# A self-planned attention and convolution kernel: ties between GpSimd and VectorE, zero matmuls in TensorE's gaps, and another schedule

## The chip, the cores and the metric

One NeuronCore of one Trainium2 chip. The metric is device time of the whole kernel in microseconds (us), the median of several executions. The kernel before took 180.95 us (179.91 to 183.62) when it was first timed.

## The reference, cut to what matters

```python
def _attn_ref(r, k, v, w, u):                 # B,H,S,D = 4,8,768,48
    for t in range(S):
        cur = np.einsum('bhd,bhe->bhde', u[None] * kt, vt)
        y[:, :, t] = np.einsum('bhd,bhde->bhe', rt, state + cur)
        state = wt[:, :, :, None] * state + np.einsum('bhd,bhe->bhde', kt, vt)

def _moe_ref(x, w_proj, filter_fft, w_out):   # x: attention's output, 4 x 768 x 384
    x1, x2, x3 = split(x @ w_proj, 3)
    x2_conv = irfft(rfft(x2) * rfft(filter_fft))      # along the sequence
    return (x1 * x2_conv * x3) @ w_out
```

Inputs are float32. The kernel computes in bfloat16 and accumulates in float32.

## The kernel before

The attention runs in 24 chunks of 128 time steps (4 batches of 6). Chunks are loaded in groups of one or two. After the six chunks of a batch comes its convolution, as discrete Fourier transforms by matmul. All four batches interleave: while TensorE transforms batch 0, the chunks of batch 1 and 2 go through.

The order of the instructions is not written by hand. Each step is an `Op` with a due time, a modelled cost for each engine that can do it, and a flag `lock`. A greedy planner chooses at each step the operation that can start first, and the kernel then emits the instructions in planned order. `lock` marks VectorE operations with two inputs in SBUF and all GpSimd operations: in the *plan* they exclude each other through the variable `port`. Nothing in the emitted program enforced that. There each engine runs its own list and waits only for its data.

```python
def dve(n, lock=False):
    h = n / 960.0 + 0.069
    return (DVE, h, h + 0.09, lock)
def pool(n, h=None):                                   # GpSimd always takes the lock
    h = h or n * 0.00228 + 0.08
    return (POOL, h, h + 0.06, True)
...
    def order(self):                                   # the planner, cut
        free = {PE: 0.8, ACT: 0.8, DVE: 0.8, POOL: 0.8, SP: 0.8}
        while ready:
            ...
                    est = max(free[e], t0 + hop, port if lock else 0.0)
            ...
            est, o, (e, hold, lat, lock), got = best
            if e == PE and est < COLD:
                hold, lat = 2 * hold, lat + hold       # half clock at the start
            o.eng, free[e], o.end = e, est + hold, est + lat
            if lock:
                port = est + hold
            ...
            out.append((est, o, e, {k: held[k] for k in o.one + o.two + o.uses}))
        return out
```

Four kinds of operation:

```python
# rk: product of r and k of a group (GpSimd or VectorE); its transposes and rx follow on TensorE
op(f"rk{gi}", T(i0, O_RK), [pool(n * C), dve(n * C, True)], lambda e, bk: mul(
    e, rk[f][:, 0:n], kr[sl][:, 1, 0:n], kr[sl][:, 0, 0:n]), r=[f"r.{sl}", f"k.{sl}"], w=[f"rk.{f}"])
# vc: v times a bonus per head (GpSimd or VectorE)
op(f"vc{gi}", T(i0, O_VC), [pool(n * C, 0.78 * n), dve(n * C, True)], ...)
# kq: VectorE, one input in PSUM, one in SBUF: no lock
op(f"kq{i}", T(i, O_KH), [dve(2 * C)], ...)
# U0..U3: products of a spectrum X with the filter's spectrum HR, HI, HG: two SBUF inputs, lock
op(f"pr{b}.{nm}.{lo}", d, [dve2(C * (hi - lo), True)] + ([pool(C * (hi - lo))] if nm in ("U1", "U3") and PP else []), ...)
...
    with tc.manual_schedule(engines={E.PE, E.Activation, E.DVE, E.Pool, E.SP}):
        for est, o, e, bk in plan.order():
            o.fn(e, bk)
```

Of the kernel before, what the change touches and what calls it, by code (L numbers as in the profile page):

```python
# [11 lines left out]
BF16 = mybir.dt.bfloat16  # L12
INT32 = mybir.dt.int32
AF = mybir.ActivationFunctionType
# [6 lines left out]
L = 128  # L21
# [8 lines left out]

PE, ACT, DVE, POOL, SP = "PE", "ACT", "DVE", "POOL", "SP"

PACE = 4.317
S2O0, S2O1, S2O2, S2O3 = 20.744, 8.77, 13.518, 14.093
S2S0, S2S1, S2S2, S2S3 = 28.784, 29.661, 40.0, 9.432
TAB, FIL, TBL = 13.024, 20.0, 7.203
WP1, WP2, WP3 = 4, 2, 4
WO, FL = 9, 3
NM, PP = 11, 1
O_MA = 7  # L40
O_MC = 5.088
COLD, TIE, PB, AB, PS = 16.0, 0.51, 1.078, 0.313, 11.871
HOP = 0.07
NP = 3
NS1 = 8 - 2 * NP
SLACK = {PE: 0.032, ACT: 0.020, DVE: 0.079, POOL: 0.014, SP: 0.0}
NBP = 10
NLD, NF, NG, NS, NO = 4, 4, 2, 2, 6
LEAD, OUTD, OUTG = -8.347, 0.5, 5
BONUS = "p" * NBP + "d" * (13 - NBP)  # L50
O_LN = 1.65
O_VB = 4.7
O_RK = 3.425
O_RKU = 5.0
O_CC = 4.43
O_RT = 2.335
O_RX = 4.34
O_CP = 1.1
O_VC = 5.289
O_CSI = -1.17  # L60
O_EN = -0.078
O_KH = 0.092
O_TR = 5.123
O_QK = 5.028
O_SC = 3.04
O_MT = 5.712
O_KV = 3.636
O_SU = 3.17
O_Y = 5.164
O_XN = 7.724  # L70
O_YT = 5.514
O_XT = 5.9
O_SD = 7.149


def act(n, sb=False):
# [33 lines left out]
class Plan:  # L110
# [43 lines left out]
            av[best[1]] = 1e9  # L154
        return t, got

    def order(self):
        free = {PE: 0.8, ACT: 0.8, DVE: 0.8, POOL: 0.8, SP: 0.8}
        port, dma = 0.0, 0.0
        avail = [0.0] * (self.npairs + self.nsingles)  # L160
        held, last, moves, out = {}, {}, [], []
        for o, k in self.after:
            o.preds.add(self.named[k])
        for o in self.ops:
            o.left = len(o.preds)
            o.wait = [p for k in o.one + o.two for p in self.gate.get(k, ()) if p is not o and k not in p.uses]
            for p in o.preds:
                p.succs.append(o)
        ready = [o for o in self.ops if not o.left]
        while ready:  # L170
            best, cands = None, {}
            for o in ready:
                t0 = max((p.end for p in o.preds), default=0.0)
                got = {}
                if o.one or o.two:
                    if any(p.eng is None for p in o.wait):
                        continue
                    at = self.place(o, avail)
                    if at is None:
                        continue  # L180
                    t0, got = max(t0, at[0]), at[1]
                opts = []
                for x in o.engs:
                    e, hold, lat, lock = x
                    hop = HOP if got or any(p.eng != e for p in o.preds) else 0.0
                    est = max(free[e], t0 + hop, port if lock else 0.0)
                    for k in o.uses:
                        if last[k][1] != e:
                            est = max(est, last[k][0] + HOP)
                    opts.append((est + lat - (min(PB, max(0.0, o.due + PS - est)) if e == POOL else AB if e == ACT else 0.0), est, x))  # L190
                fin = min(opts, key=lambda q: q[0])[0]
                for f, est, x in opts:
                    if f <= fin + TIE:
                        cands.setdefault(x[0], []).append((est, o, x, got))
            for e, cs in cands.items():
                m = min(c[0] for c in cs)
                pick = min((c for c in cs if c[0] <= m + SLACK[e]), key=lambda c: (c[1].due, c[0]))
                if best is None or pick[0] < best[0]:
                    best = pick
            est, o, (e, hold, lat, lock), got = best  # L200
            ready.remove(o)
            if e == PE and est < COLD:
                hold, lat = 2 * hold, lat + hold
            o.eng, free[e], o.end = e, est + hold, est + lat
            if lock:
                port = est + hold
            if o.bus:
                if e == SP:
                    dma = max(dma, est + 1.2) + o.bus
                    o.end = dma + 0.8  # L210
                    moves.append(o)
                else:
                    start = est + 1.4
                    for m in moves:
                        if m.end - 0.8 > start:
                            m.end += o.bus
                    dma = max(dma, start) + o.bus
                    o.end = start + o.bus + 0.3
            for k in o.two + o.one:
                held[k] = got[k]  # L220
                avail[got[k]] = 1e9
            for k in o.uses:
                self.users[k] -= 1
            for k in o.one + o.two + o.uses:
                last[k] = (max(last.get(k, (0.0, e))[0], o.end), e)
            out.append((est, o, e, {k: held[k] for k in o.one + o.two + o.uses}))
            for k in o.one + o.two + o.uses:
                if self.users[k] == 0 and k in held:
                    avail[held.pop(k)] = last[k][0]
            for s in o.succs:  # L230
                s.left -= 1
                if not s.left:
                    ready.append(s)
        assert len(out) == len(self.ops)
        return out


# [5 lines left out]
def kernel(  # L243
# [12 lines left out]
    nc = tc.nc  # L256
# [50 lines left out]
    mask_neg = sb.tile([L, L], BF16, name="mask_neg")  # L307
    ident = sb.tile([L, L], BF16, name="ident")
    ones = sb.tile([L, 1], BF16, name="ones")
    scl0 = sb.tile([L, 1], FP32, name="scl0")  # L310
    u_f = sb.tile([L, H, D], FP32, name="u_f")
    u_b = sb.tile([L, H, D], BF16, name="u_b")
# [15 lines left out]
        return pairs[bk[n]]  # L328

    def mul(e, o, a, b):  # L330
        (nc.vector if e == DVE else nc.gpsimd).tensor_mul(o, a, b)  # L331

    def copy(e, o, a):
        if e == ACT:
            nc.scalar.activation(out=o, in_=a, func=AF.Copy)  # L335
        else:
            (nc.vector if e == DVE else nc.gpsimd).tensor_copy(out=o, in_=a)  # L337

    def halves_of(x):
        v4 = x.rearrange("p (a q c) -> p a q c", q=2, c=L)  # L340
# [10 lines left out]
    def maps(e, bk):  # L351
# [15 lines left out]
            )  # L367
        nc.gpsimd.memset(fmap[:, L:L + 1], float(HALF))

    def pads(e, bk):  # L370
        nc.vector.memset(ones, 1.0)
        for t in lg:
            nc.vector.memset(t[:, :, :, D:DP], 0.0)
        for t in kq:
            nc.vector.memset(t[:, :, :, D:DP], 0.0)
# [18 lines left out]
            )  # L394

    op("masks", -9, [(POOL, 1.5, 1.6, True)], masks, w=["masks"])
    op("pads", -9, [(DVE, 0.75, 0.85, False)], pads, w=["pads"])
    op("smalls", -8, [(DVE, 0.16, 0.25, False)], smalls, w=["smalls"])
    op("table", -9, [(ACT, 1.283, 1.283, False)],
       lambda e, bk: nc.scalar.preload_act_table_set("natural_log_exp_and_others"), w=["table"])  # L400
# [489 lines left out]
                second(b)  # L890

    E = mybir.EngineType
    with tc.manual_schedule(engines={E.PE, E.Activation, E.DVE, E.Pool, E.SP}):
        for est, o, e, bk in plan.order():
            o.fn(e, bk)


# [28 lines left out]
```

## Time and profile before

| | before |
|---|---|
| time, first timing | 180.95 us, 3 runs |
| span of the profiled run | 178.5 us |
| TensorE busy | 151.0 us (85%) |
| VectorE busy | 137.8 us (77%) |
| ScalarE / GpSimd busy | 129.4 / 60.2 us |
| TensorE gaps over 0.25 us, summed from the trace | 20.7 us: 13.7 before 37 us, 6.15 between 60 and 120 us |
| half clock on record | 36.4 to 43.2 us |

In the profile PE is TensorE's matmuls, PEld its weight loads, DVE is VectorE, ACT ScalarE, POOL GpSimd and SP SyncE. The rows of 40 digits cut the span into equal slices, each digit a busy share in tenths; PEclk is the granted TensorE clock in tenths of full. A line of the timeline gives start, duration, engine, source line, operation, output <- inputs, and in brackets how long the engine stood idle before it and what it waited for.

The chain of work that ended last, by engine:

```profile
PE 61%; DVE 18%; ACT 9%; DMA 5%; issue 3%; POOL 1%; SPq 1%; ACTq 0%; DVEq 0%; POOLq 0%
```

VectorE holds 18% of the path to the end, so it is not only TensorE that binds. And two groups of VectorE instructions by source line (count, then shortest/median/longest in ns, first and last start in us, forms):

```profile
L827 DVE TENSOR_TENSOR y<-eo,g x12: 541/550/1830, 88.3 to 170.3; 128x768 bf16<-128x768 bf16 x12
L798 DVE TENSOR_TENSOR U<-X,HI x11: 345/739/2109, 79.1 to 163.8; 128x1152 bf16<-128x1152 bf16 x6, 128x384 bf16<-128x384 bf16 x5
```

One form, with a median of 550 ns and a longest of 1830 ns: the longest met GpSimd (it is one of the pair of y at 112.56 us, while two vc ran on GpSimd from 111.2 to 114.4 us). I summed over the trace how much each VectorE instruction exceeds the lower quartile of its form, counting excesses over 0.06 us. The result, 5.3 us, is called *VectorE's excess* below. It compares within one trace, and so it misses a form that occurs once. There is such a case, a fourth collision, with GpSimd's rk beside a plain copy:

```profile
74.63 1.81 POOL L331 TENSOR_TENSOR rk<-kr 128x768 bf16<-128x768 f32 x1 [6.10 <-DMA kr<-in_r_dram]
74.88 1.68 DVE L696 COPY HG<-HI 1x384 bf16<-1x384 bf16 x1 [0.21 <-ACT HI L693]
```

In b_zeros and b_ties3 (below) the same copy takes 0.25 us. With it before's excess is 6.7 us. The copies of HG are planned as part of an operation of ScalarE, so neither `lock` nor the ties know of them.

### The profile page before, as it was taken

Reading aid. Unit: us, or ns where it says so; the run is one execution under the profiler, and the core shown is the slowest. Engines: PE = TensorE matmul, PEld = TensorE weight load, DVE = VectorE, ACT = ScalarE, POOL = GpSimd, SP = SyncE. Lnnn points to the kernel's source line nnn. Section 1 sums busy time; section 2 is a strip of 40 time slices with the busy share of each in tenths; the row PEclk is TensorE's granted clock in tenths of the full one; section 3 lists DMA queues with packets and bytes.
Section 4 is the critical chain, followed back from the end, with each engine's and each line's share of the span. In section 5 each row is a group of like instructions: output and inputs, shape, how many; then the busy total and the mean of one; then the engine's idle time right before and its main releaser. Section 6 shows DMA issues by size and latency. Waiting matters only on the chain.

```text
span 178.5 us, 4574 instructions
## 1 busy us (share of the span) xinstructions
PE 151.0 (85%) x1806; PEld 96.8 (54%) x1806; DVE 137.8 (77%) x249; ACT 129.4 (72%) x218; POOL 60.2 (34%) x71
## 2 busy tenths in 40 slices
PE   0639778779999799897999689799999999999850
PEld 0419556566676576473456356466676675555220
DVE  3798677545547789899969999968898899579720
ACT  4599887774798766998778767989866874647440
POOL 6542745740632713220418006804710341002000
PEclk9999999956999999999999999999999999999997
DMA  6999798999999999899998999124000000001515
GB/s 121 202 202 214 140 209 176 200 196 200 229 189 200 317 182 210 176 183 198 212 227 172 210 305 210 34 88 180 4 0 4 0 4 0 0 0 56 214 59 208
DMA packets 106054, 26.45 MB, mean 148 GB/s; under 512 B 100528, under 2 KB 106032, under 8 KB 106032
## 3 DMA queue, kind: packets, MB, share of 16 engines
q1 hardware_dynamic: 104432, 24.98, 64.1%
q0 software_dynamic: 1600, 1.18, 4.6%
q8 instruction: 14, 0.23, 0.6%
q14 instruction: 8, 0.07, 0.1%
HBM read 22.61 MB, written 4.72 MB: 153 GB/s over the span
## 4 chain that ended last, share of the span: by engine, by line
PE 61%; DVE 18%; ACT 9%; DMA 5%; issue 3%; POOL 1%; SPq 1%; ACTq 0%; DVEq 0%; POOLq 0%
PE pair L724 7%; PE pair L762 6%; PE pair L647 5%; DVE U L798 5%; PE pair L841 4%; PE single L724 4%; PE single L511 4%; ACT pair L498 3%; PE pair L523 3%; PE pair L586 3%; DMA w<-in_w_dram 3%; PE pair L640 2%; PE pair L813 2%; DVE kq L503 2%; DMA kr<-in_r_dram 2%
## 5 line engine op out<-in xcount | busy, mean ns | idle before, releaser
L331 POOL TENSOR_TENSOR rk<-kr 128x768 bf16<-128x768 f32 (+1 forms) x13 | 22.0, 1695 | 17.4 <-DMA kr<-in_r_dram 17.4
L503 DVE TENSOR_TENSOR kq<-pair,kr 128x768 bf16<-128x768 f32 x24 | 22.6, 951 | 3.8 <-PE pair L586 1.9
L543 POOL TENSOR_SCALAR_AFFINE_SELECT mt<-mt 128x512 bf16<-128x512 bf16 x11 | 7.0, 638 | 52.7 <-ACT mt L335 46.5
L498 ACT ACTIVATE pair<-pair 128x768 f32<-128x768 f32 x24 | 19.3, 804 | 4.3 <-PE pair L494 4.0
L724 PE MATMUL pair<-xT,wproj 128*128 128x384 bf16 x96 | 18.1, 326 | 0.0
L331 POOL TENSOR_TENSOR vc<-vb,cc 128x768 bf16<-128x768 bf16 (+1 forms) x9 | 12.3, 1372 | 17.1 <-ACT cc L335 8.6
L724 PEld LDWEIGHTS <-wproj 128*128 128x128 bf16 x144 | 12.5, 97 | 9.4 <-issue 2.7
L535 DVE TENSOR_TENSOR mt<-pair,mask_excl 128x1024 bf16<-128x1024 f32 x13 | 15.8, 1214 | 1.1 <-PE pair L523 1.1
L762 PE MATMUL pair<-wproj,sd 128*128 128x384 bf16 x72 | 14.7, 343 | 0.0
L841 PE MATMUL pair<-wout,y 128*128 128x384 bf16 x72 | 13.2, 326 | 1.6 <-DVE eo L824 0.8
L335 ACT ACTIVATE ab<-pair 128x768 bf16<-128x768 f32 x12 | 9.7, 812 | 6.4 <-PE pair L762 6.4
L335 ACT ACTIVATE X<-pair 128x768 bf16<-128x768 f32 x12 | 9.7, 810 | 6.4 <-PE pair L647 5.2
L335 ACT ACTIVATE xn<-pair 128x384 bf16<-128x384 f32 x24 | 11.8, 491 | 3.1 <-PE pair L586 2.5
L491 PE MATMUL pair<-lg,mask_neg 128*128 128x384 bf16 x24 | 8.3, 346 | 6.4 <-ACT lg L439 4.2
L511 PEld LDWEIGHTS <-kq 128*128 128x128 bf16 x192 | 12.9, 106 | 1.3 <-issue 0.6
L439 ACT ACTIVATE lg<-w 128x768 bf16<-128x768 f32 (+1 forms) x13 | 10.4, 797 | 3.3 <-DMA w<-in_w_dram 3.3
L335 ACT ACTIVATE o<-pair 128x768 f32<-128x768 f32 x12 | 9.4, 810 | 4.3 <-PE pair L841 4.2
L724 PE MATMUL single<-xT,wproj 128*128 128x384 bf16 x48 | 10.4, 325 | 1.8 <-DVE xT L337 1.6
L511 PE MATMUL single<-ident,kq 128*128 128x128 bf16 x128 | 10.3, 225 | 0.3 <-ACT x L335 0.3
L335 ACT ACTIVATE ev<-pair 128x384 f32<-128x384 f32 x12 | 5.9, 490 | 6.4 <-PE pair L814 6.4
L540 DVE TENSOR_TENSOR mt<-pair,mask_excl 128x512 bf16<-128x512 f32 x11 | 7.6, 687 | 3.7 <-PE pair L523 2.3
L523 PE MATMUL pair<-qk 48*128 48x128 bf16 x192 | 9.9, 227 | 0.5 <-ACT qk L335 0.3
(132 smaller groups left out, 380.2 us busy)
## 6 DMA issues: line engine op xcount, KB each, us to landing
w<-in_w_dram SPq DMA_DIRECT2D x24, 192.0 KB, 4.1
kr<-in_k_dram SPq DMA_DIRECT2D x24, 192.0 KB, 4.6
kr<-in_r_dram SPq DMA_DIRECT2D x24, 192.0 KB, 3.9
v<-in_v_dram SPq DMA_DIRECT2D x24, 192.0 KB, 3.7
out_dram<-o SPq DMA_DIRECT2D x12, 384.0 KB, 3.3
U<-in_moe_filter_fft_dram SPq DMA_DIRECT2D x1, 1152.0 KB, 7.1
wproj<-in_moe_w_proj_dram POOLq DMA_DIRECT2D x3, 288.0 KB, 5.7
wout<-in_moe_w_out_dram POOLq DMA_DIRECT2D x1, 288.0 KB, 5.8
```

The source lines that it names most:

```text
L331: (nc.vector if e == DVE else nc.gpsimd).tensor_mul(o, a, b)
L335: nc.scalar.activation(out=o, in_=a, func=AF.Copy)
L439: op(f"ln{gi}", T(i0, O_LN), [act(n * C, True)], lambda e, bk: nc.scalar.activation(out=lg[f][:, 0:n, :, 0:D], in_=wl[sl][:, 0:n], func=AF ...
L498: nc.scalar.activation(out=p[:, :, 0:C], in_=p[:, :, 0:C], func=AF.Exp)
L503: op(f"kq{i}", T(i, O_KH), [dve(2 * C)], lambda e, bk: nc.vector.tensor_mul(kq[f][:, :, :, 0:D], two(bk, f"cs{i}")[:, :, 0:C].rearrange("p ...
L511: nc.tensor.transpose(p[:, HP * m + j, :], kq[f][:, m, 2 * j:2 * j + 2, :], ident)
L523: nc.tensor.matmul(p[:, par, j, :], qk[f][p0:p0 + D, j, :], qk[f][p0:p0 + D, HP + j, :], start=True, stop=True,)
L535: op(f"mt{i}", T(i, O_MT), [dve(1024)], lambda e, bk: nc.vector.tensor_mul(mt[s2_], scored(bk, 0, 2), _mid(mask_excl, H)), r=["masks"], w= ...
L647: nc.tensor.matmul(p, F[:, ti, c0:c0 + L], x[:, ti, :], start=(ti == 0), stop=(ti == NT - 1),)
L724: nc.tensor.matmul(p, wproj[:, cb, col0:col0 + L], xT[bx][:, cb, sl], start=(cb == 0), stop=(cb == CB - 1),)
L762: nc.tensor.matmul(two(bk, n)[:, q, 0:C], sd[q][:, cb, ti * L:(ti + 1) * L], wproj[:, cb, C:2 * C], start=(cb == 0), stop=(cb == CB - 1),)
L841: nc.tensor.matmul(two(bk, n)[:, z, 0:C], y[cb][:, t0:t0 + L], wout[:, cb, :], start=(cb == 0), stop=(cb == CB - 1),)
```

## The change

It has three parts. The planner now fills planned TensorE gaps of over 0.7 us with matmuls on a tile of zeros, meant to keep TensorE busy enough for its full clock (*zeros*: 29 matmuls in four places). At emission, a GpSimd instruction is made to wait for the last VectorE instruction that the plan has finished by its start (*ties*: in the new order, GpSimd instructions with a wait for VectorE go from 12 to 41, as the prediction counted). A tie holds one direction only: no VectorE instruction is made to wait for a GpSimd one. And the planner's constants were searched anew with both in place, which gives another interleaving (*order*). The diff, cut to its core:

```diff
-PACE = 4.317
+PACE = 3.8
+WARM = 0.7
-COLD, TIE, PB, AB, PS = 16.0, 0.51, 1.078, 0.313, 11.871
+COLD, TIE, PB, AB, PS = 5.0, 0.439, 0.991, 0.313, 12.0
-NBP = 10
-NLD, NF, NG, NS, NO = 4, 4, 2, 2, 6
+NBP = 11
+NLD, NF, NG, NS, NO = 3, 3, 2, 2, 6
 ... (some 30 more constants of the same kind)
+            if e == PE and est > free[PE] + WARM:
+                step = 0.43 if free[PE] < COLD else 0.22
+                idle = [i for i in range(self.npairs, len(avail)) if avail[i] <= free[PE]]
+                if idle and est - free[PE] > step + 0.1:
+                    n = int((est - free[PE] - 0.1) / step)
+                    x = Op("warm", 0, [(PE, n * step, n * step, False)], warm(n), (), (), (), 0.0)
+                    x.end = free[PE] + n * step
+                    out.append((free[PE], x, PE, {"warm": idle[0]}))
...
+    def warm(n):
+        def fn(e, bk):
+            for _ in range(n):
+                nc.tensor.matmul(one(bk, "warm"), wt[:, 0:L], wt, start=True, stop=True)
+        return fn
+
     def pads(e, bk):
+        nc.vector.memset(wt, 0.0)
...
-        for est, o, e, bk in plan.order():
-            o.fn(e, bk)
+        done = []
+        for est, o, e, bk in plan.order(warm):
+            got = o.fn(e, bk)
+            if e == DVE and got is not None:
+                done.append((o.end, got))
+            elif e == POOL and got is not None and not o.bus:
+                before = [x for t, x in done[-12:] if t <= est + 0.15]
+                if before:
+                    tc.add_manual_dep(got.ins, before[-1].ins.name, info, reason="port")
```

(`mul` and `copy` now return the instruction they issue, so that it can be tied.)

More of the change, by code (lines that the diff above doesn't have):

```diff
@@ L31 @@
 PE, ACT, DVE, POOL, SP = "PE", "ACT", "DVE", "POOL", "SP"
-PACE = 4.317
-S2O0, S2O1, S2O2, S2O3 = 20.744, 8.77, 13.518, 14.093
-S2S0, S2S1, S2S2, S2S3 = 28.784, 29.661, 40.0, 9.432
-TAB, FIL, TBL = 13.024, 20.0, 7.203
-WP1, WP2, WP3 = 4, 2, 4
-WO, FL = 9, 3
+PACE = 3.8
+S2O0, S2O1, S2O2, S2O3 = 20.744, 10.533, 11.762, 14.08
+S2S0, S2S1, S2S2, S2S3 = 37.166, 28.306, 40.0, 11.569
+TAB, FIL, TBL = 13.024, 20.0, 7.363
+WP1, WP2, WP3 = 4, 3, 5
+WO, FL = 8, 4
 NM, PP = 11, 1
-O_MA = 7
-O_MC = 5.088
-COLD, TIE, PB, AB, PS = 16.0, 0.51, 1.078, 0.313, 11.871
+O_MA = 4.25
+O_MC = 4.463
+WARM = 0.7
+COLD, TIE, PB, AB, PS = 5.0, 0.439, 0.991, 0.313, 12.0
 HOP = 0.07
@@ L45 @@
 NS1 = 8 - 2 * NP
-SLACK = {PE: 0.032, ACT: 0.020, DVE: 0.079, POOL: 0.014, SP: 0.0}
-NBP = 10
-NLD, NF, NG, NS, NO = 4, 4, 2, 2, 6
-LEAD, OUTD, OUTG = -8.347, 0.5, 5
+SLACK = {PE: 0.071, ACT: 0.117, DVE: 0.024, POOL: 0.002, SP: 0.0}
+NBP = 11
+NLD, NF, NG, NS, NO = 3, 3, 2, 2, 6
+LEAD, OUTD, OUTG = -9.249, 0.5, 5
 BONUS = "p" * NBP + "d" * (13 - NBP)
 O_LN = 1.65
-O_VB = 4.7
+O_VB = 4.133
 O_RK = 3.425
-O_RKU = 5.0
-O_CC = 4.43
-O_RT = 2.335
+O_RKU = 4.308
+O_CC = 4.441
+O_RT = 2.548
 O_RX = 4.34
-O_CP = 1.1
-O_VC = 5.289
-O_CSI = -1.17
-O_EN = -0.078
+O_CP = 2.398
+O_VC = 3.917
+O_CSI = -1.217
+O_EN = -0.075
 O_KH = 0.092
-O_TR = 5.123
-O_QK = 5.028
-O_SC = 3.04
-O_MT = 5.712
+O_TR = 2.647
+O_QK = 5.368
+O_SC = 3.085
+O_MT = 6.009
 O_KV = 3.636
-O_SU = 3.17
-O_Y = 5.164
-O_XN = 7.724
-O_YT = 5.514
+O_SU = 2.9
+O_Y = 5.0
+O_XN = 7.823
+O_YT = 5.4
 O_XT = 5.9
-O_SD = 7.149
+O_SD = 6.848
 def act(n, sb=False):
@@ L155, in place, with order @@
         return t, got
-    def order(self):
+    def order(self, warm):
         free = {PE: 0.8, ACT: 0.8, DVE: 0.8, POOL: 0.8, SP: 0.8}
@@ L233, in order @@
                     ready.append(s)
-        assert len(out) == len(self.ops)
+        assert all(o.eng for o in self.ops)
         return out
@@ L309 @@
     ones = sb.tile([L, 1], BF16, name="ones")
+    wt = sb.tile([L, 512], BF16, name="wt")
     scl0 = sb.tile([L, 1], FP32, name="scl0")
@@ L330, in mul @@
     def mul(e, o, a, b):
-        (nc.vector if e == DVE else nc.gpsimd).tensor_mul(o, a, b)
+        return (nc.vector if e == DVE else nc.gpsimd).tensor_mul(o, a, b)
     def copy(e, o, a):
         if e == ACT:
-            nc.scalar.activation(out=o, in_=a, func=AF.Copy)
+            return nc.scalar.activation(out=o, in_=a, func=AF.Copy)
         else:
-            (nc.vector if e == DVE else nc.gpsimd).tensor_copy(out=o, in_=a)
+            return (nc.vector if e == DVE else nc.gpsimd).tensor_copy(out=o, in_=a)
     def halves_of(x):
@@ L396 @@
     op("masks", -9, [(POOL, 1.5, 1.6, True)], masks, w=["masks"])
-    op("pads", -9, [(DVE, 0.75, 0.85, False)], pads, w=["pads"])
+    op("pads", -9, [(DVE, 0.95, 1.05, False)], pads, w=["pads"])
     op("smalls", -8, [(DVE, 0.16, 0.25, False)], smalls, w=["smalls"])
@@ L892 @@
     E = mybir.EngineType
+    info = mybir.DependencyInfo(mybir.DependencyClass.Sync, mybir.DependencyReason.SCHED_ONLY)
     with tc.manual_schedule(engines={E.PE, E.Activation, E.DVE, E.Pool, E.SP}):
-        for est, o, e, bk in plan.order():
-            o.fn(e, bk)
+        done = []
[7 more added lines that the diff above has]
+                    tc.add_manual_dep(got.ins, before[-1].ins.name, info, reason="port")
 _INS = ['r', 'k', 'v', 'w', 'u', 'moe_w_proj', 'moe_filter_fft', 'moe_w_out']
```

## The prediction

> **What bounds the kernel now.** I read the page first: engine totals, then the 40 slices.
>
> ```profile
> PE 151.0 (85%) x1806; PEld 96.8 (54%) x1806; DVE 137.8 (77%) x249; ACT 129.4 (72%) x218; POOL 60.2 (34%) x71
> ...
> PE   0639778779999799897999689799999999999850
> ...
> PEclk9999999956999999999999999999999999999997
> DMA  6999798999999999899998999124000000001515
> ```
>
> A slice is 4.46 us. TensorE is busy nearly everywhere from slice 9 on (about 37 us). DMA is full until slice 24 (107 us) and then nearly idle. So two stages bind: at the start TensorE waits for loads, later it has a backlog and is the bound. I looked for the border in GpSimd's timeline: in the early stage its product rk of r and k starts within 0.3 us of the landing of r for groups 2, 3 and 4 (17.4, 27.6, 36.0 us); from group 5 on, k has landed 7 to 30 us before VectorE's kq reads it (for example 44.9 against 52.0). So before about 37 us a faster TensorE only waits longer for a load; after it, each microsecond of TensorE saved should be a microsecond of the end.
>
> The clock row has two low slices. I asked for TensorE by windows of 3.41 us laid on the recorded change at 36.39 us (columns: us, busy, granted clock, DMA share, GB/s):
>
> ```profile
> 29.56:32.98 3.42, 3.42 (x55) 1.00 0.79 151
> 32.98:36.39 3.41, 1.82 (x31) 1.00 1.11 207
> 36.39:39.80 3.41, 2.86 (x36) 0.50 1.24 200
> 39.80:43.22 3.42, 3.42 (x25) 0.50 1.09 203
> 43.22:46.63 3.41, 3.41 (x40) 1.00 1.10 215
> ```
>
> One window in which TensorE was busy for only 1.82 of 3.41 us is followed by two at half clock. The timeline confirms it by durations: six 384-column matmuls take 2.13 us at 39.97 us and 1.15 us at 48.03 us. The same signature shows that the start is cold too, though the record shows a 1.00 clock there: eight transposes of kq take 1.03 us at 7.55 and 1.06 us at 13.87, but 0.62 us at 22.45. The first recorded change is at 19.3 us.
>
> Third, I looked for VectorE instructions much longer than others of their form. Three stand out, and the timeline shows GpSimd beside them:
>
> ```profile
> 93.48 1.82 POOL L331 TENSOR_TENSOR rk<-kr 128x768 bf16<-128x768 f32 x1
> ...
> 93.76 2.16 DVE L798 TENSOR_TENSOR U<-X,HR 128x1152 bf16<-128x1152 bf16 x1 [0.23 <-ACT X L335]
> ...
> 95.38 2.04 POOL L331 TENSOR_TENSOR rx<-rk,u_b 128x768 bf16<-128x768 bf16 x1
> ...
> 95.92 2.11 DVE L798 TENSOR_TENSOR U<-X,HI 128x1152 bf16<-128x1152 bf16 x1
> ...
> 101.23 0.65 PE L724 MATMUL single<-xT,wproj 128*128 128x384 bf16 x3 [1.61 <-DVE xT L337]
> ...
> 103.63 0.32 PE L491 MATMUL pair<-lg,mask_neg 128*128 128x384 bf16 x1 [0.41 <-DVE kq L503]
> ```
>
> The products U, about 0.74 us each elsewhere, take 2.16 and 2.11 us while GpSimd runs. TensorE then sits idle for 1.61 and 0.41 us behind the late VectorE. At 112.56 us a pair of products y takes 2.29 us (two others: about 1.1) beside GpSimd's vc, and TensorE loses 0.76 us before L841 waiting for VectorE's mt.
>
> [...] kq (PSUM and SBUF) keeps 935 to 959 ns in all 24 cases.
>
> **The change, part by part.** (1) *Matmuls on zeros.* The planner puts 512-column matmuls of a zero tile into planned TensorE gaps over 0.7 us. The built order has 29 of them: 8 before the first real matmul, 7 after the first cumulative sums, 11 before the second transposes of kq, 3 before the transposes of the fifth chunk or so; none later. At the warm rate seen here (six of 384 columns start about 0.97 us apart from the next group, so 0.16 us each) one costs 0.16 x 512/384 = 0.215 us, an estimate, and twice that cold: 6.2 to 12.5 us of matmul, all where TensorE now idles (4.17, 1.72 and 2.65 us gaps before 13.3 us). At the start they can save about half of the cold work there: the first 19 us hold about 7 us of it on the chain, hence 2 to 3 us locally. But the next stage waits for loads that land at 17.2, 27.4 and 35.9 us whatever TensorE does, so I credit 0 to 0.5 us of this. (2) *The mid dip.* If the clock holds from 36.39 to 43.22, the work of 6.83 us at half clock takes 3.4 us, and here there is a backlog, so 3.4 us reach the end. No zero matmuls lie directly there; the gain needs the retuned order, or an earlier, fuller TensorE, to avoid the half-empty window. I give it three in five: 2.0 us, with the small start credit 2.3 us.
>
> (3) *Ties.* Without its tie lines the changed kernel has the same order on every engine, but only 12 GpSimd instructions wait for VectorE; with them 41 do. They keep GpSimd from running ahead into a VectorE product planned before it. At stake is the idle time of TensorE behind the three collisions: 1.61 + 0.41 + 0.76 = 2.8 us (of 4.1 us of VectorE time: 1.42 + 1.37 + 1.28). The planner already serializes the two in its plan, so the ties should remove most: 0.7 x 2.8 = 2.0 us. Cost: a late VectorE now delays GpSimd. GpSimd is busy 34% and most of its waits are slack, but rk in the load-bound stage has none; I charge 0.5 us.
>
> (4) *Another schedule.* TensorE's real instructions are the same in number but for six more transposes of rk and six small matmuls (about 0.5 us, as one bonus group moves from VectorE to TensorE). VectorE sheds about 1.7 us: two U products of 0.74 go to GpSimd and one comes back, two vc of 0.95 and one reduction of 0.95 leave, two rk of about 0.95 arrive (an estimate from equal-sized products). The interleaving is new: batch 1's projections come earlier, the tail after the last forward transform is the same. Buffers for loads go from 4 sets to 3. Group 8's k was read last at 102.6 us, so group 11's k, issued at 92.9 us now, must wait for it; but group 11 is not read until 127.6 us, so that should be hidden. All loads are now issued ahead of all stores. I credit a retuned order 1.5 us, a guess rather than a count.
>
> Sum: 180.95 - 2.3 - 2.0 + 0.5 - 1.5 = 175.7; rounded to **175.5 us**.
>
> **Rivals.** *A: the clock still dips.* The stage from 17 to 36 us is bound by loads, with TensorE 69 to 78% busy in its windows, and only three zero matmuls come near it. Another half-empty window gives the 3.4 us back, perhaps at another place, and matmuls on zeros might not be counted as activity. For it: [...] the three runs before spread from 179.91 to 183.62. Then about 178.5 us. *B: the ties become the wait.* GpSimd stands still for a VectorE that waits for TensorE, rk and vc come late, and y waits for vc. For it: 29 new waits, and the early rk starts are bare of slack. Against: the tied instruction is always one planned to be finished. Then 179 to 183 us. *C: the load-bound start is longer*, since three buffer sets stop the queue: for it, DMA is full until 107 us, and a hole there moves everything; against, early sets are read within 1 to 8 us of landing. Then 179 to 182 us. *D: everything holds*, the dip is gone, all collisions are gone, and the order fills TensorE in the middle: 180.95 - 3.4 - 2.8 - 4 = about 170.5 us.
>
> **Range and chances.** D sets the low side with some room for a better order, A with a part of B the high one: **169.5 to 180.5 us**. Two per cent is 3.6 us, so faster means under 177.3. It needs either both main gains at about half, or one whole and a better order: 0.67. Within 2%: 0.28. Slower: 0.05, for B or C in full.
>
> **What would show it.** Right: the clock row stays at 9 from the third slice on and the eight transposes of kq take about 0.6 us before 10 us; no 1152-wide U or y above about 1 us in VectorE's groups; TensorE's gaps between 60 and 120 us fall from about 6 us to 3; rk's wait for r stays in the early stage. Wrong on the clock: two slices of 5 or 6 again. Wrong on the ties: GpSimd's waits for VectorE lead the list and ScalarE or TensorE wait for vc or rk. Wrong on the start: PE's first backlogged stretch begins later than 37 us. The prediction fails altogether if TensorE, from 37 to 165 us, has as many gaps as now, because the new order has made others.

## The result, and the profile after

The changed kernel took 172.36 us (171.13 to 173.03, 4 runs) against 180.81 us (179.91 to 183.62, 4 runs) for the kernel before: ratio 0.954, 95% interval 0.946 to 0.962. All runs of the changed kernel were fast. The ratio comes out only if 183.62 us, 2% above the fastest, is left out as slow (the other three have a mean of 180.51, the changed kernel one of 172.22). The ratio here and below is the mean time of one kernel's fast runs over that of the other's fast runs of the same rounds, so it is not quite the ratio of the medians.

The same file was timed twice more with the experiments: 175.81 us (ratio 0.9642) and 174.13 us (0.9532), with before at 182.61 and 182.21. All three lie in the predicted range. These two ran on one and the same chip; which chip the first timing ran on is not recorded, so it is called *the first timing* below.

From the page of the changed kernel, its totals and the slices that answer to those in the prediction:

```profile
PE 153.4 (91%) x1845; PEld 94.5 (56%) x1847; DVE 131.1 (77%) x247; ACT 129.0 (76%) x219; POOL 59.7 (35%) x72
...
PE   7986867899999989999999999999999999999860
...
PEclk9999999999999999999999999999999999999997
DMA  5999999999999899989999998967000000002516
```

The clock row has no low slice, and from slice 16 (about 64 us) TensorE is at 9 until its tail, where before it dipped to 6 and 7. DMA is busy until slice 28 (about 118 us), where before it thinned out after slice 25 (about 112 us). VectorE lost 6.7 us of busy time. Its share of the chain fell from 18% to 4%:

```profile
PE 66%; ACT 13%; SPq 8%; DVE 4%; issue 3%; DMA 3%; ACTq 0%; DVEq 0%
```

The same groups by source line as before:

```profile
L844 DVE TENSOR_TENSOR y<-eo,g x12: 549/552/559, 93.7 to 161.7; 128x768 bf16<-128x768 bf16 x12
L815 DVE TENSOR_TENSOR U<-X,HI x9: 351/427/751, 83.8 to 155.2; 128x384 bf16<-128x384 bf16 x5, 128x1152 bf16<-128x1152 bf16 x4
```

No y takes over 559 ns and no such U over 751 ns. (One collision is left: a U with HR of 1148 ns at 81.7 us.) VectorE's excess is 1.3 us instead of 5.3. The start, in TensorE's timeline:

```profile
1.24 3.60 PE L383 MATMUL single<-wt 128*128 128x512 bf16 x8 [1.24 <-DVE wt L387]
...
5.42 2.33 PE L383 MATMUL single<-wt 128*128 128x512 bf16 x7
...
7.76 0.61 PE L528 MATMUL single<-ident,kq 128*128 128x128 bf16 x8
```

Eight zero matmuls take 3.60 us, 0.45 us each, twice the 0.22 us between the starts of the last of the next seven: the array is cold. Seven take 2.33 us, 0.33 each, through the change to the full clock at 6.8 us. The first eight transposes of kq then take 0.61 us; in the kernel before they took 1.03 us.

**Where the time came from.** To see in which stage it was won I added up the real matmuls (zeros left out) that had started by a given time, each at its full-clock cost. The cost is an estimate from the traces of before and of the changed kernel: where TensorE runs one matmul after another at full clock, the step from start to start is most often 162 ns for 384 columns, 82 ns for 192, 56 ns for 128, and 25 ns for 48, 8 or 1. (The sums were made with values within 1 ns of these; that moves them by about 0.1 us in these two traces.) Matmuls that the trace shows in pairs, starting a few ns apart on parts of the array, count half. The whole kernel has about 130 us of such work. How the paired ones are counted moves all rows alike, by up to 3 us, and the differences between rows by under 0.6 us.

| profiled run | timing | us | work by 60 us | work from 60 to 120 us |
|---|---|---|---|---|
| before | first | 180.22 | 35.1 | 47.6 |
| changed kernel | first | 171.13 | 38.1 | 52.7 |

By 60 us the changed kernel is 3.0 us of work ahead, and it gains another 5.1 us by 120 us. Together that is most of the 9.1 us between these two runs. Two separate causes are to be looked for: one early, one in the middle.

### The profile page after: what moved, and what is told of

Its sections match the earlier page's. It is cut to its first block, busy times and chain, and to the rows that moved or that the text cites. A ratio compares the mean times of both kernels' runs of the same rounds, so it can differ in the third digit from the quotient of the medians.

```text
span 169.4 us, 4679 instructions
## 1 busy us (share of the span) xinstructions
PE 153.4 (91%) x1845; PEld 94.5 (56%) x1847; DVE 131.1 (77%) x247; ACT 129.0 (76%) x219; POOL 59.7 (35%) x72
## 4 chain that ended last, share of the span: by engine, by line
PE 66%; ACT 13%; SPq 8%; DVE 4%; issue 3%; DMA 3%; ACTq 0%; DVEq 0%
PE pair L741 10%; SPq L447 7%; PE pair L779 7%; PE pair L664 6%; PE pair L858 5%; PE single L741 4%; PE single L528 4%; PE pair L657 3%; PE pair L540 3%; DMA u_f<-in_u_dram 3%; PE pair L603 3%; ACT pair L515 2%; PE pair L830 2%; PE single L618 2%; PE pair L826 2%
## 5 line engine op out<-in xcount | busy, mean ns | idle before, releaser
L341 POOL TENSOR_TENSOR vc<-vb,cc 128x768 bf16<-128x768 bf16 (+1 forms) x11 | 14.9, 1356 | 22.0 <-DVE cc L347 12.4
L515 ACT ACTIVATE pair<-pair 128x768 f32<-128x768 f32 x24 | 19.3, 806 | 2.9 <-PE pair L511 1.8
L341 POOL TENSOR_TENSOR rk<-kr 128x768 bf16<-128x768 f32 (+1 forms) x11 | 18.4, 1669 | 6.9 <-DVE xT L347 1.9
L552 DVE TENSOR_TENSOR mt<-pair,mask_excl 128x1024 bf16<-128x1024 f32 x13 | 15.8, 1219 | 2.7 <-PE pair L540 2.7
L341 POOL TENSOR_TENSOR U<-X,HI 128x1152 bf16<-128x1152 bf16 (+1 forms) x3 | 5.6, 1878 | 25.0 <-DVE rk L341 12.6
L779 PE MATMUL pair<-wproj,sd 128*128 128x384 bf16 x72 | 13.7, 326 | 0.5 <-ACT cc L345 0.4
L456 ACT ACTIVATE lg<-w 128x768 bf16<-128x768 f32 (+1 forms) x13 | 10.4, 801 | 3.6 <-DMA w<-in_w_dram 3.6
L528 PEld LDWEIGHTS <-kq 128*128 128x128 bf16 x192 | 11.4, 97 | 2.5 <-DVE kq L520 1.6
L528 PE MATMUL single<-ident,kq 128*128 128x128 bf16 x144 | 11.0, 219 | 0.8 <-DVE kq L520 0.7
L345 ACT ACTIVATE qk<-single 128x1024 bf16<-128x1024 bf16 x10 | 10.2, 1022 | 0.7 <-PE single L528 0.7
L383 PE MATMUL single<-wt 128*128 128x512 bf16 x27 | 8.8, 483 | 1.6 <-DVE wt L387 1.2
```

Source lines behind the costliest of these rows:

```text
L341: return (nc.vector if e == DVE else nc.gpsimd).tensor_mul(o, a, b)
L345: return nc.scalar.activation(out=o, in_=a, func=AF.Copy)
L456: op(f"ln{gi}", T(i0, O_LN), [act(n * C, True)], lambda e, bk: nc.scalar.activation(out=lg[f][:, 0:n, :, 0:D], in_=wl[sl][:, 0:n], func=AF ...
L515: nc.scalar.activation(out=p[:, :, 0:C], in_=p[:, :, 0:C], func=AF.Exp)
L528: nc.tensor.transpose(p[:, HP * m + j, :], kq[f][:, m, 2 * j:2 * j + 2, :], ident)
L552: op(f"mt{i}", T(i, O_MT), [dve(1024)], lambda e, bk: nc.vector.tensor_mul(mt[s2_], scored(bk, 0, 2), _mid(mask_excl, H)), r=["masks"], w= ...
```

## The experiments

Theory: the early gain is the clock (zeros), the middle gain is the collisions of VectorE and GpSimd (ties), and the order adds a little. Rivals: the order alone does it, the ties and zeros being trimmings; or the zeros are enough, since VectorE's delays are hidden behind TensorE's backlog.

Every kernel is the changed file with small edits. "Old order" means before's constants put back (checked: the same instruction order as before on every engine, apart from the clearing of the zero tile). Zeros off is `range(0)`, ties off is `if False`. All results were correct.

| label | order | zeros | ties | median us (range, runs) | before | ratio [95%] |
|---|---|---|---|---|---|---|
| b_zeros | old | yes | no | 182.62 (181.42–183.25, 4) | 182.4 | 1.001 [0.994, 1.008] |
| b_ties | old | no | yes | 177.2 (175.49–178.72, 4) | 182.4 | 0.9689 [0.961, 0.977] |
| b_both | old | yes | yes | 175.53 (175.21–175.7, 4) | 182.4 | 0.9632 [0.957, 0.969] |
| a_order | new | no | no | 179.19 (177.59–180.19, 4) | 182.4 | 0.9821 [0.975, 0.990] |
| a_zeros | new | yes | no | 177.22 (176.41–179.64, 4) | 182.61 | 0.9708 [0.965, 0.977] |
| a_ties | new | no | yes | 176.58 (175.22–177.87, 4) | 182.61 | 0.9711 [0.965, 0.977] |
| a_all | new | yes | yes | 175.81 (175.18–176.22, 4) | 182.61 | 0.9642 [0.960, 0.968] |
| b_ties3 | old | no | 4 only | 178.39 (177.85–178.6, 4) | 182.61 | 0.9782 [0.974, 0.982] |
| a_all_again | new | yes | yes | 174.13 (173.81–175.26, 6) | 182.21 | 0.9532 [0.948, 0.958] |
| a_more | new | +13 | yes | 172.94 (172.53–173.54, 6) | 182.21 | 0.9466 [0.943, 0.950] |
| a_start | new | first 15 | yes | 176.78 (175.77–177.39, 6) | 182.21 | 0.9669 [0.961, 0.973] |
| b_both_again | old | yes | yes | 176.14 (175.16–177.09, 6) | 182.21 | 0.9639 [0.958, 0.970] |

The rows are three calls of four (equal values of before belong together). The first call ran on one chip, the other two shared another. One run each of b_ties (178.72), a_zeros (179.64) and a_ties (177.87) counted as slow and is left out of its ratio, and so is one of before in the first call (183.32) and one in the third (183.3). The profiled run of b_ties is that slow one, so its trace is not used in the comparisons below.

### Call 1: each part on the old order, and the bare order

```diff
 b_ties:          for _ in range(n):      ->  for _ in range(0):
 b_zeros:         if before:              ->  if False:
 b_both:          neither
 a_order:         both, with the new constants
 (b_*: constants of before)
```

> The kernel before, its own order, with the zero matmuls alone (36 of them, put by the same rule into its own planned TensorE gaps, the zero tile and its memset added; no ties). Theory 'clock' (each part brings what it was sized at): the dip at 36 to 43 us is gone from the clock row and the time falls by about 3.4 us, to 177.4. Rival 'order' (the retuned schedule does nearly all, the rest is decoration): 180 to 181, dip gone or not. Rival 'not counted' (zeros are no activity for the clock): first recorded change still near 19 us and the dip stays, about 181.

> The kernel before, its own order, with the ties alone. Theory 'clock and ties as sized': the three long VectorE products (2.16, 2.11 us U, 1.8 us y) go back to 0.75 and 0.55 us and the time falls by about 2.8 us less 0.5 us for new GpSimd waits, to 178.5; the clock dip stays. Rival 'order': 180.5 to 181.5. Rival 'ties become the wait': 182 or more.

> The kernel before, its own order, with zero matmuls and ties. Theory 'clock and ties as sized': the two savings add, about 175. Rival 'order': about 180. Rival 'parts need each other': both alone bring nothing and together about 176.

> The changed kernel's order with neither zero matmuls (the planner plans the same, none is issued) nor ties. Theory 'clock and ties as sized': it loses about 6 us of the 8.4 gained, so about 178. Rival 'order': about 173.

*b_zeros* gained nothing (1.001), although 36 zero matmuls (the old order has other gaps) brought the clock up at 5.1 us and the dip at 36 us is gone. Its clock row shows the new dip in slices 4 and 5 and full clock after it:

```profile
PEclk9997599999999999999999999999999999999998
```

So where did the gain go? VectorE's excess in b_zeros is 8.9 us, against 5.3 before. VectorE's and GpSimd's timelines at the place of before's worst collision:

```profile
95.44 2.29 DVE L815 TENSOR_TENSOR U<-X,HI 128x1152 bf16<-128x1152 bf16 x1
97.65 2.39 DVE L341 TENSOR_TENSOR vc<-vb,cc 128x768 bf16<-128x768 bf16 x1
```

```profile
94.69 2.41 POOL L341 TENSOR_TENSOR rk<-kr 128x768 bf16<-128x768 f32 x1 [0.26 <-DMA kr<-in_r_dram]
97.18 2.04 POOL L341 TENSOR_TENSOR rx<-rk,u_b 128x768 bf16<-128x768 bf16 x1
```

The collision moved to other instructions (a U and a vc in place of two U's), a new one came at 68.9 us (the filter sums fsd, 1.62 us too long), and the rk that met one copy of HG in before meets the next one at 76.6 us (1.52 us too long). The y at 114.2 us still takes 1.83 us. Nothing in the program says who goes first, so with other timing other pairs meet. What was given back was small, though. The clock was low again from 15.4 to 22.2 us, and at 60 us b_zeros is only 0.4 us of work ahead of before (another timing; table below). By 120 us it is 1.0 us behind. So most of the forecast 3.4 us was never there to lose.

*b_ties* took 3.1% off by itself. *b_both* took 3.7%: with the ties in place, the zeros seem worth about 0.6%, though the two intervals overlap. In b_both's trace one collision got past the ties: r of a group landed at 87.9 us and released its rk at 88.25 us, and a y that started just after took 2.18 us beside it (excess 3.1 us; 1.3 in b_both_again). *a_order* (0.9821, verdict unclear at 2%) has an excess of 6.2 us: the new order by itself does not avoid collisions. Of the forecasts, b_both's about 175 us held; b_ties (178.5) and b_zeros were wrong as said, and a_order was 1.2 us slower than theory's 178.

### Call 2: each part on the new order, and four ties alone

```diff
 a_zeros:         if before:              ->  if False:
 a_ties:          for _ in range(n):      ->  for _ in range(0):
 a_all:           the changed kernel
 b_ties3:         if before:              ->  if before and o.name in ('rk10', 'rku10', 'vc9', 'vc10'):
 (b_ties3: constants of before, zeros off)
```

> The changed kernel without ties: its order and its 29 zero matmuls. In the order of before, zeros alone gave nothing and ties alone about 3%, so theory 'ties first' (what the zeros win is lost again to collisions that move): 178 to 179.5, clock row full from about 7 us, several VectorE instructions 1 us or more too long. Theory 'clock' (3.4 us for the clock wherever it dips): 175.5.

> The changed kernel without zero matmuls: its order and its ties. Theory 'ties first': the ties take 5 us off the 179.2 of the bare order, so 174; the start and some windows run cold. Theory 'clock': 176.

> The changed kernel itself, unchanged, on the same chip as the two that lack a part. Ratio to before 0.954 as in the first measurement, with both theories; it is the anchor of the comparison.

> The kernel before with only four ties: on rk and rx of group 10 and vc of groups 9 and 10, the GpSimd instructions that stood beside the three long VectorE products. Theory 'the three collisions are the gain': nearly all of the gain of all ties, so about 177.5, with the two U near 0.75 us. Theory 'ties work everywhere' (many small displacements): less than half of it, 179.5 or more, and collisions elsewhere.

*b_ties3* is the sharpest test of the cause. It ties only the GpSimd instructions of the three collisions that the prediction named: rk and rx of group 10, and vc of groups 9 and 10. The time fell by 2.2% of 182.61 us, that is 4.0 us (its verdict at 2% is unclear, since the interval reaches 0.982, but it excludes 1). The sum of what VectorE lost in these collisions in the trace of before is 1.42 + 1.37 + 1.28 = 4.07 us. That the two agree so closely is partly chance. b_ties3 has other collisions, 1.24 us at 68.8 us (fsd) and 1.37 us at 77.4 us (before's fourth, in another copy of HG), and its profiled run is only 1.75 us below that of before (178.47 and 180.22 us, different timings). The stage by engines, in before and then in b_ties3 (us, then busy us and number of PE, PEld, DVE, ACT and POOL, clock, DMA share, GB/s):

```profile
93.00:105.00 12.00, 9.98 (x113) 6.45 (x111) 11.77 (x14) 9.38 (x14) 4.34 (x3) 1.00 1.01 199
```

```profile
93.00:105.00 12.00, 12.00 (x145) 7.73 (x144) 10.49 (x17) 11.12 (x18) 4.10 (x3) 1.00 0.99 192
```

In before VectorE is busy for 11.77 of 12 us with 14 instructions, and TensorE for 9.98. With the four ties VectorE does 17 instructions in less time and TensorE is never idle. So VectorE was the bound of this stage, and its "busy" time contained the wait for GpSimd. In work as counted above, b_ties3 comes to 93 us about 1.7 us behind before, after the collisions at 68.8 and 77.4 us, and is 1.6 us ahead at 120 us. Between these it gains 3.3 us, most of the 4.07. The first 60 us of b_ties3 are like before's (35.1 us of work in both, though before's trace is from the first timing).

*a_zeros*, *a_ties* and *a_all* ran in the same rounds: 0.9708, 0.9711, 0.9642. On the new order each of zeros and ties adds about 0.7% (1.2 us) to the other; the intervals overlap, so this is a size with wide edges. VectorE's excess is 6.2 us in a_zeros, and 1.3 in the two with ties. So 4.9 us of excess went for 1.2 us of time. Part of the reason is the clock: all four runs of a_all list clocks of 0.964 to 0.968, the three fast ones of a_zeros 0.975 to 0.987. In the table below a_all gains 3.3 us on a_zeros in the middle and is 2.5 us behind at 60 us. From a_order to a_ties the same 4.9 us of excess brings 1.9 us in the middle. Lost VectorE time is thus not always repaid in full, and whether the ties have a part in a_all's longer dip is open. Of the forecasts, a_zeros (178 to 179.5) and a_ties (174) fit theory 'ties first' badly: 177.2 and 176.6 us, and a_ties is where the rival 'clock' had it (176). b_ties3 fell between its two (177.5 and 179.5).

All traces side by side, in the measure of the table above:

| profiled run | ties | work by 60 us | work from 60 to 120 us | half clock after the first rise, us |
|---|---|---|---|---|
| b_zeros | no | 35.5 | 46.2 | 15.4–22.2 |
| a_zeros | no | 36.9 | 48.9 | 24.2–27.6, 119.7–123.2 |
| a_order | no | 34.4 | 50.3 | 20.7–30.9 |
| b_both | yes | 36.0 | 51.9 | 13.3–16.7 |
| b_both_again | yes | 35.6 | 52.0 | 14.4–21.2 |
| a_ties | yes | 34.8 | 52.2 | 20.7–24.1 |
| a_start | yes | 33.6 | 52.0 | 12.6–16.0, 19.5–29.7 |
| a_all | yes | 34.4 | 52.2 | 19.3–29.5 |
| a_all_again | yes | 34.7 | 52.3 | 18.4–28.7 |
| a_more | yes | 37.0 | 52.2 | none |
| changed kernel, first timing | yes | 38.1 | 52.7 | none |

The middle column splits by the ties: 46.2 to 50.3 us without them, 51.9 to 52.7 with all of them, whatever the order, the zeros or the chip (the four ties of b_ties3 give 49.2, and the slow run of b_ties about 50.6, just above a_order). The early column varies with the clock: the two runs without a dip lead, and a_zeros with a short one is just behind. On the way to these 52 us the order and the ties seem to do the same job: the bare new order gains 2.7 us here over before, while next to zeros and ties it gains 0.2 to 0.4 us (a_all and a_all_again over b_both and b_both_again).

### Call 3: how many zeros, and why the later timings are slower

The changed kernel kept its clock in the first timing and lost it in call 2, at about 19 us. TensorE by windows of 3.41 us laid on the recorded clock changes (the half clock stretches in the table last one, two or three times that: 3.4, 6.8 and 10.2 us), first timing (us, busy, clock, DMA share, GB/s):

```profile
10.21:13.63 3.42, 2.69 (x26) 1.00 1.06 210
13.63:17.04 3.41, 2.01 (x45) 1.00 1.01 199
17.04:20.45 3.41, 2.89 (x55) 1.00 0.95 177
```

and in a_all:

```profile
12.43:15.84 3.41, 2.67 (x48) 1.00 1.02 205
15.84:19.26 3.42, 1.60 (x19) 1.00 0.74 158
19.26:22.67 3.41, 3.10 (x41) 0.50 0.98 207
```

The first timing's emptiest window is 59% busy (2.01 us) and the clock holds. In a_all it is 47% (1.60 us), and 10.2 us at half clock follow. In the first timing r of group 2 landed at 15.8 us, here at 17.6 us, so TensorE had less to do at that time. Hence the test: put zeros where these windows are thin, in any PSUM bank that the plan has free, or take away all zeros but those at the start.

```diff
 a_more:
+MORE = {'sc1': 5, 'rt2': 4, 'sc4': 4}
+            if e == PE and o.name in MORE:
+                bank = min((avail[i], i) for i in range(len(avail)) if i not in got.values())
+                if bank[0] < est:
+                    x = Op("warm", 0, [(PE, 0.0, 0.0, False)], warm(MORE[o.name]), (), (), (), 0.0)
+                    x.end = free[PE]
+                    out.append((free[PE], x, PE, {"warm": bank[1]}))
 a_start:         for _ in range(n):      ->  for _ in range(n if n in (8, 7) else 0):
 a_all_again:     the changed kernel
 b_both_again:    as b_both
```

> The changed kernel itself again, as the anchor for this chip. The first measurement gave 0.954 of before with a full clock row, the second (another chip) 0.964 with ten microseconds at half clock from 19.3 us, after a window that was 47% busy because loads came 1.8 us later. Theory 'window': the ratio follows the clock row, 0.954 where it is full and 0.964 where it dips. Theory 'chip': the ratio differs with no dip to show for it.

> The changed kernel with zero matmuls at three more places where both its profiles show TensorE waiting: 5 before the scores of chunk 1, 4 before the turn of rk of group 2, 4 before the scores of chunk 4. Theory 'window': the window from about 16 to 19.3 us stays over 60% busy even with late loads, no dip, and the time is 172 to 173 whatever the chip, at most equal to the changed kernel where that has no dip, 3.5 us better where it has. Rival 'they only delay': the zeros stand before work that was ready, the time is 0.5 to 1.5 us worse.

> The changed kernel with only the first 15 zero matmuls (before 6 us); the 11 and the 3 later ones left out. Theory 'window': a warm start alone is hidden by the loads; without the later ones a window between 9 and 20 us falls under 55% busy, the clock dips, and the time is that of the kernel with no zeros, about 176.5. Rival 'the start is what counts': as the changed kernel.

> The old order with both additions, now beside the changed kernel on one chip: what is left between the two is the retuned schedule alone. From the bare orders (0.982) and the first measurement, theory 'the parts add' expects the retuned schedule to be worth 1.8%, 3 us. From the two calls so far (0.9632 and 0.9642, different chips) rival 'the order is worth nothing once the other two are in' expects less than 0.5%.

*a_more* runs at 172.94 us, 0.9466 of before; a_all_again in the same rounds is at 0.9532. The two intervals touch, but no run of one lies in the range of the other (172.53 to 173.54 and 173.81 to 175.26). In these rounds it is faster than both given kernels. Its windows:

```profile
13.83:17.24 3.41, 2.93 (x38) 1.00 0.93 185
17.24:20.65 3.41, 3.41 (x48) 1.00 0.78 175
20.65:24.07 3.42, 2.75 (x60) 1.00 1.02 202
```

r of group 2 landed at 17.6 us here too, and yet the clock holds: none of these windows is below 80% (the one before them, from 10.4 us, has 79%). The clock rows of a_all, a_more and a_start:

```profile
PEclk9999756999999999999999999999999999999998
```

```profile
PEclk9999999999999999999999999999999999999999
```

```profile
PEclk9996756999999999999999999999999999999997
```

*a_start*, with only the 15 zeros at the beginning, is at 0.9669. That is the level of a_ties without any zeros (0.9711, in other rounds; the intervals overlap widely). The full clock comes at 5.8 us instead of 17.3, and the end doesn't notice: the clock falls again at 12.6 us, and rk has to wait for loads anyway. The two traces differ later, too: a_start spends 13.6 us at half clock, a_ties 3.4. But at 12.6 us, where a_start's first dip begins, both have done 2.1 us of work. A warm start by itself is not worth a measurable amount here; keeping the clock until the loads are ahead is worth 1.4% (a_start to a_all_again) to 2.0% (to a_more).

Only one run of a label is traced, but the record lists the granted clock of every run, and times follow it. In a_all all four runs list 0.964 to 0.968, that is 11 to 12 us at half clock with the end included (an estimate from span and clock). In a_all_again only the profiled run does (0.966, 175.26 us, its slowest); the other five list 0.975 to 0.985, that is 5 to 9 us, and take 173.8 to 175.0 us. This is the same kernel on the same chip, and it explains why a_all_again came out at 0.953, where its forecast, made from traces, had 0.964 for a run with a dip. a_more lists 0.980 for its slowest run (173.54) and 0.993 to 1.000 for the rest. Its forecast (172 to 173 us) and that of a_start (about 176.5) came true.

This chip also shows a cost of the ties. GpSimd's timeline in a_all_again and in a_more, rk of groups 3 and 4:

```profile
28.44 1.82 POOL L341 TENSOR_TENSOR rk<-kr 128x768 bf16<-128x768 f32 x1 [0.40 <-DVE m L347]
...
39.00 1.81 POOL L341 TENSOR_TENSOR rk<-kr 128x768 bf16<-128x768 f32 x1 [1.86 <-DVE xT L347]
```

```profile
27.67 1.81 POOL L348 TENSOR_TENSOR rk<-kr 128x768 bf16<-128x768 f32 x1 [1.28 <-DMA kr<-in_r_dram]
...
37.46 1.81 POOL L348 TENSOR_TENSOR rk<-kr 128x768 bf16<-128x768 f32 x1 [2.23 <-DMA kr<-in_r_dram]
```

In a_all_again r landed at 26.5 and 36.1 us, but the tied rk started 1.9 and 2.9 us later, released by VectorE, which was late itself behind a half-clock TensorE. In a_more it starts within 0.2 us of the landing. A lost clock is thus passed on by the ties. How much of the end this costs was not measured apart from the clock.

*a_all_again* against *b_both_again*, the order with all else in place, is 0.9532 to 0.9639, or 1.1% (2.0 us). But a_all of call 2 and b_both of call 1 stand at 0.9642 and 0.9632. And the two profiled runs of call 3 are 175.26 and 175.59 us, too near each other for their traces to show where 2 us would lie. The order's worth beside the others is between nothing and 2 us, and stays open; neither forecast (1.8%, or less than 0.5%) was met.

## Why the prediction was right or wrong

The time was right (175.5 us predicted; 172.36, 175.81 and 174.13 us measured), and so were the two main mechanisms. The terms of the sum were not all of the right size, and it is partly luck that the total came near: the ties were credited with far too little, the clock on the old order with too much, and the order's term covers time that the ties save as well.

- **"TensorE's idle time behind three collisions is at stake": the mis-sized term.** The prediction took 0.7 x 2.8 = 2.0 us. The ties alone give 3.1% of 182.4 us, or 5.7 us, on the old order, and the four ties of the named collisions alone 4.0 us. It had the right number in hand, "4.1 us of VectorE time", and set it aside for TensorE's gaps. But in that stage VectorE was busy for 11.77 of 12 us: it was the bound, and most of what it lost there reached the end (3.3 us of work gained between 93 and 120 us in b_ties3). The other 1.7 us (an estimate across two chips) are probably the collisions that four ties leave: b_ties3 still has an excess of 3.7 us, with 1.24 us at 68.8 and 1.37 us at 77.4 us, where b_both_again has 1.3 us in all. The prediction's "three stand out" also missed the copy of HG, 1.43 us too long. In full is no rule, though: on the new order 4.9 us of excess brought 1.9 to 3.3 us of work.
- **The clock, 2.3 us.** On the old order it measured 0.0 us without ties and about 0.6% (1 us) with them; on the new order 0.7% (1.2 us) for the 29 zeros and 2.0% from 15 zeros to 42 (a_start to a_more). The three-in-five chance that the dip goes was fair for the one at 36 us, but the prediction thought of one dip. The dip moved rather than vanished: in all profiled runs of the experiments that have zeros or the new order, save a_more, it came back between 12 and 31 us. So rival A came true for the changed kernel itself in the profiled runs of both later timings, at 174 to 176 us instead of its 178.5. Its ground was misread in part: of the five windows from 19 to 36 us three were 69 to 78% busy, one was full, and the last had the 53% that cost the clock.
- **The start, 0 to 0.5 us,** was right, and for the reason given: a_start shows a warm start that gains nothing measurable.
- **The waits made by the ties, 0.5 us (rival B).** The waits are there: GpSimd's longest in the changed kernel are for VectorE (one of 12.6 us before a U), but almost all of it is slack. The early rk was named as the place without slack, and that is where they show, 1.9 and 2.9 us, when the clock is down. In the first timing GpSimd stood 1.86 us idle for VectorE before rk of group 4 too, 1.2 us of it after r had landed at 34.9 us, and the kernel was still at its fastest.
- **The order, 1.5 us, "a guess rather than a count".** Bare it gave 1.8% (3.3 us; the verdict is unclear), beside the others 0 to 2.0 us. It was called a guess, and remains one; the part in the middle seems to be the same time that the ties save.
- **Rival C, a longer load-bound start from three buffer sets,** did not come: the last r landed at 110.4 us (112.7 before), and the early slices of DMA are as full as they were. (Before's DMA row is full for 25 slices, to 112 us, and not 24 and 107 us as the prediction read it; nothing rests on it.)
- **The signs.** Clock at 9 throughout and kq at 0.61 us: seen in the first timing, not in the later ones for the clock. No y or wide U above 1 us: seen, but for one of 1.15 us. TensorE's gaps between 60 and 120 us from 6 to 3 us: they went from 6.15 to about 2. No engine waited over 0.53 us for a GpSimd rk or vc.

## What to carry to other kernels

When a plan assumes that two instructions exclude each other, put that order into the program with a semaphore: otherwise a gain elsewhere changes which of them collide, as b_zeros shows (an excess of 8.9 us against 5.3), and may be lost again. A tie in one direction leaves the other open, as the y in b_both shows (2.18 us beside an rk), and a plan knows only of the collisions that it models: the copies of HG were not among them. Size the worth of a removed collision first by the engine that was the bound in its stage, with its own lost time as the most that can come back, not by the idle gaps of the engine that leads over the whole span: here 4.07 us of lost VectorE time and, partly by chance, 4.0 us won, against gaps of 2.8 us. Zero matmuls paid here where TensorE was warm and thinly fed by loads, until the loads were ahead (172.94 us in a_more, 174.13 in a_all_again, 176.78 in a_start); look at the busy share of each window of 3.41 us, in more than one timing, since the landing of loads moves it (59% in the first timing, 47% in a_all).

## What the traces show of the clock and the collisions

- In the 14 traces, the end of the kernel left out, the clock fell 15 times, after windows of 3.41 us that were 7 to 70% busy, 12 of them under 60% (53% in before, 47% in a_all, 44% in a_all_again and in b_zeros). No window above 71% was followed by a fall. Of 19 warm windows under 60%, 12 were. What decides for the other seven (45 to 60% busy, one of 59% in the changed kernel) is open.
- Matmuls on zeros bring the clock up here: the full clock came at 4.1 to 7.1 us in the nine profiled runs with zeros at the start and at 16.8 to 19.3 us without. Whether transposes help to keep it, no run was made to tell. The traces lean towards yes: without them the window of a_all from 39.7 us is only 26% busy and that of the changed kernel from 27.3 us 28%, and both kept the clock, while b_ties3 lost it after a window with 58% of other matmuls.
- A warm start gained nothing measurable (a_start, 0.9669 of before, against a_ties, 0.9711, in other rounds). A dip later on has a cost: a_more, which has none, is 0.7% faster than a_all_again, whose profiled run has 10.2 us at half clock, and 2.0% faster than a_start.
- A VectorE product U of two SBUF inputs, 0.74 us elsewhere, took 2.16 us in before beside GpSimd's rk. Four waits of GpSimd on VectorE saved 4.0 of 182.6 us.
- The clock record is silent about a cold start: before shows clock 1.00 in its first windows, yet eight transposes take 1.03 us there and 0.62 us later, and the first record is at 19.3 us. So the mean clock that a run lists flatters kernels with a cold start.
